# Another list of orders and engines for the operations of a Nyström attention followed by a ReLU MLP

## The chip, the cores and the metric

The kernel runs on one core of one Trainium2 chip. The metric is the device time of one execution in microseconds (us). The time before is 260.32 us, the median of three runs (260.05, 260.32 and 260.85).

## The reference

Inputs are q, k and v of shape 8 batches x 8 heads x 576 positions x 64, all float32, then a gain vector of 512 and two weight matrices, 512 x 2048 and 2048 x 512. Cut to what matters:

```python
q_lm = q.reshape(B, H, 32, 18, D).mean(axis=3)      # 32 landmarks
k_lm = k.reshape(B, H, 32, 18, D).mean(axis=3)
A  = softmax(scale * q @ k_lm^T)                    # 576 x 32
Bm = softmax(scale * q_lm @ k_lm^T)                 # 32 x 32
C  = softmax(scale * q_lm @ k^T)                    # 32 x 576
Z  = Bm^T / (norm1(Bm) * norminf(Bm) + 1e-6)
for _ in range(6):
    Z = 2 * Z - Z @ Bm @ Z
x   = A @ Z @ C @ v                                 # then heads side by side: 576 x 512
xn  = (x - mean(x)) / sqrt(var(x) + 1e-6) * g_ln
out = x + relu(xn @ w_ch1) @ w_ch2
```

## The kernel before, in words

The kernel does not issue its instructions as it builds them. Its functions record 1,649 operations (class `Op`), each with one engine or a choice of engines, in groups of batches: the start with batch 0 (operations 0 to 277), then the sets (1), (2), (3), (4, 5) and (6, 7) in `SETS`. A string `ORDER` then lists all operation numbers in the order of issue, and a string `BY` gives one letter (P for GpSimd, A for ScalarE, D for VectorE, S for SyncE's queue) for each operation that has a choice. A loop at the end issues them; each engine works through its own part of this order, and waits by semaphores for what it needs.

```python
    by = [op.by if len(op.by) == 1 else next(ways) for op in program]
    for i in order:
        program[i].issue(by[i])
```

Tiles are named buffers of a `Place` with a few slots. `Buf.place` takes the first free slot when an operation that uses the tile is issued, and `done` gives it back after the last one, so that the order of the list sets the rotation of the slots also. Loads land in `stg` (6 slots); results of matmuls stand in PSUM as `bank` (4 slots) or as `p` (pairs of banks, 2 slots).

For each batch, q, k and v come in halves (four heads each, 576 KB): a load (line 231, on SyncE's queue), a cast to fp16 on one of three engines (line 201, into `nat` for q and k, `natv` for v), and for q and k a turn, which is a transposing DMA (line 827, SyncE's queue, into `xT`). Landmarks of k come from sums of the cast tile on GpSimd (`asum`, `s`) and a small product on TensorE; landmarks of q come from reduces on VectorE over the turned tile (line 835). Then follow the scores of the landmarks, their softmax, the six iterations on 32 x 32 tiles (`st`), the scores of k and q with exponentials on ScalarE (`ect`, `ea`; `e` in the profile), their normalization by a multiplication with `lns` (e<-e,lns), and the product with v (`cv`). `zt` is the small product of the iterated matrix and `cv`; copied out of PSUM it lets TensorE form `m`, which takes the first layer of the MLP directly from `ea` (p<-e,m). The relus of the first layer (`hT`) run on ScalarE (line 210) or VectorE (line 211). Sums of hT tiles (`mix`, line 214) go to VectorE or GpSimd and feed the second layer, whose parts VectorE adds to the residual in `xblk` (line 217); stores follow on SyncE's queue.

Matmuls of one set are woven with the second layer of the set before. The operations of batch 7, which the change and the text on it speak of, are: 1294 and 1296 the loads of k, 1295 and 1297 their casts, 1298 and 1299 their turns; 1300 to 1303 and 1305 to 1308 GpSimd's sums for the landmarks of k; 1304 and 1309 TensorE's products of these; 1311 and 1313 the loads of q, 1312 and 1314 their casts, 1315 and 1316 their turns; 1317 and 1318 the reduces, 1319 the mask, 1324 the landmark scores; 1320 and 1322 the loads of v. Beside them run, for batches 4 and 5, 1001 and 1005 (e<-e,lns), 1007 and 1009 (copies of zt), 1038 and 1042 (the matmuls that need 1001 and 1005), 1057 to 1059 (copies of m), 1060 to 1075 (products p<-e,m, each with its relu). Of set (2), 481 and 483 are the loads of q, 482 and 484 their casts.

Of the kernel before, what the change touches and what calls it, by code (L numbers as in the profile page):

```python
# [20 lines left out]
def kernel(  # L21
# [1128 lines left out]
    for n, bs in enumerate(SETS):  # L1150
# [9 lines left out]
        0-1 14 2-6 9 15 52 17 10 16 18 11 19 55 21 12 20 22-23 58 25 13 24 27 26 28 61 29-30 7 32 34  # L1160
        31 40 35 41 33 36 43 37 63 38 42 8 39 45-46 44 103 47-48 104 107 66 49 53 101 108 102 109 54
# [5 lines left out]
        89 281 80 285 224 290 282 182 214 186 91 278 183 286 82 211 188 291 287-288 93 187 84 234  # L1167
# [4 lines left out]
        332 567 329 492 242 256 468 333 317 257 318 467 258 334 319 259 482 320 330 260 335-336 679  # L1172
# [3 lines left out]
        571 681 485-486 682 487 274 369 488 392 480 385 356 686 409 393 489 410 687 386 275 398 500  # L1176
        688 353 399 502 690 494 501 411 495 420 503 691 421 394 692 390 693 422 579 423 570 572 696
        698 254 705 265 683-684 697 707 496 400 699 497-499 395 890 391 706 701 504 357 522 689 505
        694 346 424 524 506 695 507 412 350 523 508-509 533 892 359 354 534 403 358 700 510 413 404
# [4 lines left out]
        438 901 583 910 556 442-443 749 902 444 547 582 704 920 596 750 911 598 597 917 445 751 554  # L1184
        446-447 439 599 588 565 922 557 548 589 448 895 449 903 549 717 569 450 715 718 709 453 550
        716 904 429 454 919 710 900 590 711-712 584 551 591 555 713 578 455 937 585 921 905 586 912
        714 456 587 906 744 926 457 558 745 719 600 720 594 939 927 721-722 603 559 419 723-724 923
# [4 lines left out]
        758 982 631 640 1266 638 981 632 767 771 942-943 768 641 763 642 764 754 637 752 647 753 646  # L1192
        755 772 759 440 648 643 760 644 990 994 761 991 649-650 645 995 653 949 996 958 651 781 959
        652 654 782-783 1265 1281 655 784 765 659 656 1267 1283 791 658 799 769 792 1270 1290 660
        657 800 1268 789 944 661 1271 790 797 1272 795 773 798 775 1273 945 662 796 1275 787 776 666
        785 663 788 669 1282 1276 786 950 960 1285 951 801 961 952 670 1284 762 953 804 954 766 793
        955 1269 770 1277 774 671 777 803 997 964 794 962 965 802 821 778 966-967 963 1286 672 811
        992 673 968 807 812 993 969-970 1274 808 1292 813 971 244 1278 676 972 805 814 973 451 1287
        822 806 462 809 667 974 817 810 975 668 823 833 818 1294 824 1288 779 835 819 780 827 820
        1279 815 826 976 825 986 816 977 834 978 828 987 1291 836 988-989 829-830 979 1293 1296 839  # L1200
# [8 lines left out]
        1325-1326 1082 1026 1093 1327-1328 1050 1030 1097 1329 1083 1051 1094 1036 1098 1095 1090  # L1209
        1044 1031 1338 1091 1084 1339 1032 1340 1099 1110 1341 1085-1086 1100 1087 1342 1334 1343  # L1210
        1336 1037 1335 1112 1102 1344 1046 1345 1337 886 1080 887 1346 1360 1081 1347 889 1109 888
        1348 1103 1361 1111 865 1362-1363 1104 875 1105 1349 1101 1354 1041 1350 1047 1106 1355 1113
# [72 lines left out]
```

## Time and profile before

| | us |
|---|---|
| median of three runs | 260.32 |
| the profiled execution | 259.61 |
| its span | 257.9 |
| TensorE (PE) busy | 248.5 (96%) |
| VectorE (DVE) busy | 201.8 (78%) |
| ScalarE (ACT) busy | 175.1 (68%) |
| GpSimd (POOL) busy | 161.8 (63%) |
| DMA engines, q1, share of 16 engines' span | 71.7% |

The span is that of the profiled instructions; the time of the profiled execution is 1.7 us more. TensorE's clock was granted at 0.999 of full speed. A row of the timeline or of the groups gives the engine, the line of the code, the operation and the tiles (out<-in); bracketed parts give the idle time ahead of it and what ended that. SPq is SyncE's queue, on which DMAs are issued in order.

### The profile page before, as it was taken

To read this page: it belongs to the slowest core of one execution; us is meant where nothing else is said; L and a number is where in the kernel's file an instruction comes from. 1 tells how busy PE (TensorE), PEld (TensorE's weight loads), DVE (VectorE), ACT (ScalarE), POOL (GpSimd) and SP (SyncE) were. 2 spreads that over 40 slices of the span, in tenths; PEclk is the share of its full clock that TensorE was granted. 3 is DMA by queue.
4 is the path that set the end of the run, shared out by engine and by line. 5 is a ranking of instruction groups with operands and counts; after the bars stand their busy time and mean duration, and the time that the engine had idled before them with its cause. 6 is when DMAs were issued, how large, how long until landed. Compare 5 with 4: busy or idle time off the path is not lost.

```text
span 257.9 us, 7929 instructions
## 1 busy us (share of the span) xinstructions
PE 248.5 (96%) x3241; PEld 178.3 (69%) x3241; DVE 201.8 (78%) x436; ACT 175.1 (68%) x298; POOL 161.8 (63%) x172
## 2 busy tenths in 40 slices
PE   7799999999999999999999899999999999999994
PEld 6644865456654668877778556768777885788882
DVE  2678997799887889898797969799768867776651
ACT  2598987998998789989879477567776434643000
POOL 6278764899999986999382592795356007406810
PEclk9999999999999999999999999999999999999999
DMA  6999999999999999999989995020060013000646
GB/s 242 378 403 397 403 409 406 351 319 294 259 296 320 276 294 360 269 253 246 214 254 267 237 191 158 22 66 3 4 142 21 4 29 75 0 3 20 159 106 185
DMA packets 51788, 53.73 MB, mean 208 GB/s; under 512 B 30628, under 2 KB 30888, under 8 KB 51752
## 3 DMA queue, kind: packets, MB, share of 16 engines
q1 hardware_dynamic: 51352, 52.70, 71.7%
q10 hardware_dynamic: 400, 0.52, 0.7%
q8 instruction: 25, 0.41, 0.6%
q14 instruction: 11, 0.09, 0.1%
HBM read 36.70 MB, written 9.44 MB: 179 GB/s over the span
## 4 chain that ended last, share of the span: by engine, by line
PE 80%; DMA 10%; POOL 5%; SPq 2%; ACT 1%; issue 1%; DVE 0%; POOLq 0%; ACTq 0%
PE bank L194 50%; PE p L194 30%; DMA stg<-in_v_dram 3%; DMA stg<-in_moe_w_ch_dram 3%; DMA stg<-in_q_dram 3%; POOL asum L214 2%; SPq L231 2%; DMA out_dram<-xblk 1%; POOL natv L201 1%; PE p L198 1%; POOL w L379 1%; POOL e L214 0%; ACT natv L201 0%; POOL nat L201 0%; ACT lns L205 0%
## 5 line engine op out<-in xcount | busy, mean ns | idle before, releaser
L194 PE MATMUL bank<-w,hT 128*128 128x256 f16 (+3 forms) x496 | 89.2, 311 | 0.0
L210 ACT ACTIVATE hT<-p 128x576 f16<-128x576 f32 x102 | 64.5, 651 | 31.1 <-PE p L194 30.6
L194 PE MATMUL p<-e,m 128*128 128x288 f16 x512 | 79.2, 286 | 0.2 <-ACT lns L205 0.2
L194 PEld LDWEIGHTS <-hT 128*128 128x128 f16 x688 | 63.7, 98 | 20.5 <-issue 3.4
L194 PEld LDWEIGHTS <-m 128*128 128x128 f16 x512 | 48.4, 98 | 17.7 <-issue 2.0
L217 DVE SCALAR_TENSOR_TENSOR xblk<-bank,rstd,xblk 128x256 f32<-128x256 f32 (+2 forms) x97 | 46.7, 506 | 16.6 <-PE bank L194 15.3
L214 POOL TENSOR_TENSOR mix<-mix,hT 128x1024 f16<-128x1024 f16 x10 | 21.6, 2169 | 22.0 <-DVE mix L214 20.0
L194 PE MATMUL bank<-stg,mix 128*128 128x256 f16 x192 | 25.4, 273 | 0.0
L549 DVE BATCH_NORM_STATS2 six<-xblk 128x6 f32<-128x512 f32 x36 | 24.4, 682 | 0.9 <-ACT xblk L201 0.9
L205 ACT ACTIVATE e<-p 128x576 f16<-128x576 f32 x32 | 19.7, 652 | 7.5 <-PE p L194 7.2
L211 DVE TENSOR_SCALAR hT<-p 128x576 f16<-128x576 f32 x26 | 19.4, 753 | 6.1 <-PE p L194 5.7
L214 POOL TENSOR_TENSOR e<-e,lns 128x576 f16<-128x576 f16 x11 | 14.4, 1316 | 15.5 <-ACT lns L205 8.4
L214 POOL TENSOR_TENSOR hT<-hT 128x1024 f16<-128x1024 f16 x6 | 12.8, 2128 | 14.9 <-DVE mix L214 14.9
L194 PEld LDWEIGHTS <-mix 128*128 128x128 f16 x192 | 18.2, 98 | 3.9 <-issue 1.3
L201 ACT COPY xblk<-bank 128x512 f32<-128x512 f32 (+2 forms) x30 | 17.0, 582 | 3.8 <-PE bank L194 3.7
L201 POOL CAST natv<-stg 128x1152 f16<-128x1152 f32 x8 | 10.4, 1310 | 11.5 <-DMA stg<-in_v_dram 8.3
L201 POOL CAST nat<-stg 128x1152 f16<-128x1152 f32 x12 | 14.2, 1196 | 4.8 <-DMA stg<-in_q_dram 3.0
L201 DVE CAST nat<-stg 128x1152 f16<-128x1152 f32 x12 | 10.4, 866 | 8.7 <-DMA stg<-in_q_dram 7.3
L835 DVE TENSOR_REDUCE qlm<-xT 128x64 f16<-128x1152 f16 x12 | 16.0, 1344 | 1.1 <-DMA xT<-nat 1.1
L214 POOL TENSOR_TENSOR asum<-asum 128x256 f32<-128x256 f32 (+1 forms) x24 | 15.4, 642 | 1.3
L214 POOL TENSOR_TENSOR asum<-nat 128x512 f32<-128x512 f16 x12 | 14.8, 1236 | 1.0 <-ACT nat L201 0.5
L201 ACT CAST m<-p 128x1024 f16<-128x1024 f32 x11 | 11.2, 1014 | 5.9 <-PE p L194 5.8
(124 smaller groups left out, 411.3 us busy)
## 6 DMA issues: line engine op xcount, KB each, us to landing
stg<-in_q_dram SPq DMA_DIRECT2D x16, 576.0 KB, 6.4
stg<-in_k_dram SPq DMA_DIRECT2D x16, 576.0 KB, 6.0
stg<-in_v_dram SPq DMA_DIRECT2D x16, 576.0 KB, 5.9
out_dram<-xblk SPq DMA_DIRECT2D x67, 128.0 KB, 3.5
stg<-in_moe_w_ch_dram SPq DMA_DIRECT2D x16, 512.0 KB, 6.8
xT<-nat SPq DMA_TRANSPOSE x24, 6.3
out_dram<-xblk ACTq DMA_DIRECT2D x3, 128.0 KB, 2.8
out_dram<-xblk ACTq DMA_DIRECT2D x1, 96.0 KB, 2.7
```

What stands on the lines that cost most here:

```text
L194: PE(lambda e, o, l, r: e.matmul(o, l, r, start=start, stop=stop, tile_position=(rb, cb), skip_group_check=(skip or cb != 0)), o, l, r)
L198: PE(lambda e, o, l, r: e.matmul(o, l, r, is_transpose=True, tile_position=(0, 0)), o, i_, idn)
L201: later(by, lambda e, o, i: e.copy(o, i) if e is nc.scalar else e.tensor_copy(out=o, in_=i), o, i)
L205: later("A", lambda e, o, i: e.activation(o, i, func, **kw), o, i)
L210: later(by, lambda e, o, i: e.activation(o, i, AF.Relu) if e is nc.scalar else e.tensor_scalar(out=o, in0=i, scalar1=0.0, scalar2=None, op ...
L211: e.tensor_scalar(out=o, in0=i, scalar1=0.0, scalar2=None, op0=ALU.max), o, i)
L214: later(by, lambda e, o, x, y: e.tensor_tensor(out=o, in0=x, in1=y, op=op), o, x, y)
L217: later("D", lambda e, o, x, s, y: e.scalar_tensor_tensor(out=o, in0=x, scalar=s, in1=y, op0=op0, op1=op1), o, x, scalar, y, hold=hold)
L231: later(by, lambda e, o, i: e.dma_start(out=o, in_=i), o, i)
L379: e.tensor_scalar(out=o, in0=i, scalar1=g, scalar2=0.0, op0=ALU.mult, op1=ALU.add),
L549: later("D", lambda e, o, i: e.bn_stats(out=o, in_=i), six, x_blk[j])
L835: later("D", lambda e, o, i: e.tensor_reduce(out=o, in_=i, axis=AX.XY, op=ALU.add), t[:, x, :], xT[x].rearrange("p j (g a) -> p g j a", a=2))
```

## The change

Only the two strings are replaced. `ORDER` lists the same 1,649 operations in another order (one line more, so that later lines count one higher), and `BY` changes the engine of 93 of them: for example 15 relus of hT go from VectorE to ScalarE and 11 the other way, 3 casts of q or k from VectorE to GpSimd and 3 back, 3 multiplications by lns from VectorE to GpSimd and 4 the other way. Its author describes it as a new list from a replay with turns placed when their issue ends, and with loads that may take buffers four places ahead. In the stretch that holds batch 7's loads of q, 1312 goes from VectorE to GpSimd, 1314 from GpSimd to ScalarE, 1005 from GpSimd to VectorE, 1007 from VectorE to ScalarE, and 1009 from ScalarE to VectorE. The core of the diff:

```diff
     ORDER = """
-        0-1 14 2-6 9 15 52 17 10 16 18 11 19 55 21 12 20 22-23 58 25 13 24 27 26 28 61 29-30 7 32 34
-        31 40 35 41 33 36 43 37 63 38 42 8 39 45-46 44 103 47-48 104 107 66 49 53 101 108 102 109 54
+        0-1 14 2-6 9 15 52 17 10 16 18 11 19 55 21 12 20 22 278 23 58 25 13 24 27 26 28 61 29-30 7
+        32 34 31 40 35 41 33 36 43 37 63 38 42 8 39 45-46 44 103 47-48 104 107 66 49 53 101 108 102
...
-        831 452 1010 1280 983 837 665 832 840 1013 984 1311 1011 841 677 985 1012 847 1014 1295 675
-        842 1289 1002 678 843 1027 848 1003 844 664 998 838 1028 1015 1313 849 1016 845 674 850 999
-        1019 1298 852-853 1297 846 854 1008 851 1006 1023 1004 1312 855 1009 856 1000 1320 1007 1017
-        859 1299 1020 860 1001 1024 1332 1021 1330 1333 858 861 1314 857 1331 862 1315 1056 866 1005
-        869 1018 1059 1057 870 1058 1300 871 1316 872 1025 1062 863 1301 1042 873 1063 1038 1070 876
-        1302 1029 868 879 1071 1303 880 877 1305 1039 1072 867 1043 1066 1073 1322 1033 1306 881
-        1067 1022 874 1034 1064 1321 1035 864 1317 1060 1065 878 1304 882 1307 1061 1076 1318 1308
-        883 1079 1068 1309 884 1319 1069 1310 1074 1077 1088 1075 1078 1324 885 1089 1040 1323 1092
+        839 1293 1296 830 677 983 831 837 1010 1311 840 985 832 668 1011 841 984 1012 674 842 1013
+        1295 847 664 844 1002 1014 848 451 1003 838 1019 665 998 843 1020 1027 849 1313 845 999 850
+        1298 1289 1028 853 851 1297 1023 1312 852 1008 1006 854 846 855 1024 1300 1299 856 1004 1009
+        859 858 1007 1000 1015 1021 860 1016 1301 1330 857 1332 1315 1005 1331 861 1302 1333 862
+        1001 1056 1314 869 1059 1058 870 1303 1316 871 1057 1305 872 866 863 1072 876 1306 1038 1073
+        1070 1017 1320 879 1307 1322 873 1071 1042 1039 1308 865 1064 1043 880 1317 864 1065 1033
+        1062 875 878 881 1034 1063 1025 1060 877 1304 1066 1035 1061 874 1318 882 1067 1309 1068
+        1310 883 1069 1319 884 1018 1076 1022 1324 1074 1077 1079 1321 1029 885 1325 1090 1075 1036
...
     BY = """
-        PPPPPAAPPPPPPPDPPPPDPPDPADAAPAAAPADDDAAADDADADPADAAAADDAADDAADADDAADDAAAADADAAPPADAAAADDAD
-        DPDADAAADAAAADDAAAADADAAAAAAAADDDDDPDPDPADDDAAAAAAAAADPAAAAAAADAAAAAAAAAAAAAAAAAAAAADDPPPD
-        DDAPADDAPAPAPAAPPPPPDAAAAADDAADDAADAAAAAADADDAAAAAAAAADPPPPPDPDDADAADDAAAADAAAAAAAADPDDPDD
-        DPPPDDPAAAADDPPPPPPPADADDADADAAADDAAAADDDADADAAAAAADDADDPPPDDDADAAAAAADAAADADAADAADADDPPDP
-        PPSSASSSAASASA
+        PPPPPAAPPPPPPPDPPPPPPPDAADAAPAAAPADDADADADAAAPDDDDDAADDAAADAADAADAADDAAAADADAAPDAPAAAADDAD
+        DPPADADADADAADAAAADDADAAAAAAAAAADDDPPPDDADDDAAAAAAAAAPPAAAAAAAAAAAAAADAAAAAAAAAAAAAADDPPPD
+        DDAAADPAAPDADDAPPPPDADAAAADDDAADAADAAAAAAAADAAAAAAAAADDPPPPDPDDDAAAADAADADDAAAAAAAAADDDDPD
+        PPPPADPAAAAAPAPPPDPDAADAAADDAADADDAAADAADADADAADDDADAADDPPPPPDAAADADAADAADAAADAAAAAADDPPPD
+        DDASASSAASSASA
     """
```

More of the change, by code (lines that the diff above doesn't have):

```diff
@@ L1195 @@
[L1195 to L1199, printed above, removed]
@@ new lines @@
+        1359 1386 1052 1173 1370 1130 1385 1174 1388 1167 1371 1126 1168 1163 1387 1128 1389 1164
+        1372 1127 1397 1131 1390 1373 1169 1122 1132 1170 1045 1376 1134 1393 1377 1135 1049 1133
+        1171 1398 1165 1378 1172 1136 1394 1053 1145 1166 1374 1137 1379-1380 1382 1375 1146 1381
+        1383 1054 1159 1175 1160 1138 1177-1178 1161 1176 1147 1162 1142 1193 1055 1139 1181 1194
+        1391 1140 1148 1182-1183 1144 1149 1195 1152 1141 1184-1185 1392 1153 1179 1186 1154 1196
+        1180 1430 1143 1197 1207 1151 1433 1191 1431 1150 1201 1432 1192 1187 1395 1412 1188-1189
@@ new lines @@
+        1209 1198 1190 1401 1200 1446 1402 1208 1434 1447 1420 1199 1202 1435 1403 1203 1210 1442
+        1204 1212 1443 1213 1205 1220 1440 1206 1438 1421 1441 1214 1396 1413 1439 1215 1436 1211
+        1221 1437 1450 1222 1452-1453 1216 1219 1444 1451 1218 1223 1217 1462 1445 1224 1463 1227
+        1226 1228 1399 1454 1400 1458 1225 1455 1407 1229 1409 1230 1459-1460 1408 1233 1231 1456
+        1404 1232 1405 1234 1457 1235-1236 1461 1448 1483 1243 1529 1237 1487 1244 1240 1449
+        1245-1246 1253 1247 1485 1468 1250 1249 1254 1469 1251 1255 1530 1256 1238 1532 1471 1252
@@ new lines @@
+        1257 1406 1464 1248 1258 1465-1466 1410 1259 1467 1260 1414 1531 1472 1411 1261 1473 1541
+        1484 1416 1542 1537 1422 1488 1474 1417 1538 1547 1418 1477 1548 1424 1476 1543 1425 1486
+        1415 1475 1478 1544 1479-1480 1419 1426 1533 1470 1545 1534 1489 1481 1490 1495 1482 1491
[3 rows of a table added]
+        1520 1586 1560 1263 1521-1522 1515 1581 1569 1518 1526 1583 1570 1523 1239 1571-1572 1517
+        1575 1573 1242 1576 1574 1585 1527 1577-1578 1241 1587 1580 1524 1588 1579 1262 1589 1593
+        1590 1528 1595 1591 1596 1592 1597 1594 1598 1601 1599 1602 1600 1603-1604 1607 1606 1608
@@ L1238 @@
+        1605 1609-1610 1617 1614 1618 1611 1615-1616 1619 1612 1620 1627 1621 1628 1624 1629 1622
+        1630 1625 1631 1626 1632 1623 1525 1633-1634 1613 1638-1639 1635 1640-1645 1637 1636 1646
+        1648 1647
     """
     BY = """
[L1240 to L1242 removed]
```

41 lines of the change are left out of this document (11 added, 30 removed), and 70 rows, old and new, of the table ORDER.

## The prediction

> **What bounds the kernel now.** I read the page first (engine shares), then the windows, then the waits, and last the timeline around the largest wait.
>
> ```profile
> span 257.9 us, 7929 instructions
> PE 248.5 (96%) x3241; PEld 178.3 (69%) x3241; DVE 201.8 (78%) x436; ACT 175.1 (68%) x298; POOL 161.8 (63%) x172
> ```
>
> TensorE (PE) works 96% of the span. The other engines have room on average, so what a reordering can win is mostly the time in which TensorE stands still. The windows say where that is (columns: window, its length, then busy time and instructions of each engine, granted clock, DMA share, GB/s).
>
> ```profile
> core 0: us, PE busy (x) PEld busy (x) DVE busy (x) ACT busy (x) POOL busy (x), PEclk, DMA share, GB/s
> 25.00:140.00 115.00, 115.00 (x1565) 77.87 (x1562) 101.45 (x215) 100.63 (x173) 92.05 (x89) 1.00 1.07 307
> 140.00:145.00 5.00, 3.86 (x78) 3.13 (x62) 3.41 (x6) 3.73 (x8) 1.28 (x1) 1.00 1.11 224
> 145.00:150.00 5.00, 4.88 (x51) 3.23 (x50) 4.57 (x10) 2.40 (x5) 4.07 (x4) 1.00 1.06 232
> 150.00:155.00 5.00, 4.93 (x60) 2.58 (x58) 3.48 (x6) 3.76 (x7) 4.61 (x8) 1.00 1.19 192
> 155.00:160.00 5.00, 4.69 (x43) 3.41 (x44) 4.93 (x14) 3.31 (x8) 1.42 (x2) 1.00 0.61 191
> 180.00:210.00 30.00, 29.85 (x318) 23.38 (x317) 22.86 (x43) 18.73 (x32) 9.91 (x6) 1.00 0.16 37
> 237.00:257.90 20.90, 17.02 (x156) 14.43 (x154) 9.21 (x20) 0.65 (x1) 6.32 (x3) 0.99 0.58 145
> ```
>
> From 25 to 140 us TensorE has no gap at all. From 140 to 160 it lacks 1.14 + 0.12 + 0.07 + 0.31 = 1.64 us, from 180 to 210 another 0.15. The last window's 3.88 us are the time after the last matmul. The start, up to 25 us, has its own waits:
>
> ```profile
> engine line waited for: us in total, times, longest us
> PE bank L194 <- DVE zeros L254: 1.5, 1, 1.5
> PE p L198 <- DVE nat L201: 1.2, 2, 0.9
> PE p L194 <- DVE zt L201: 1.1, 1, 1.1
> PE bank L194 <- POOL s L214: 0.4, 1, 0.4
> ```
>
> Zeros and nat belong to the start. The zt row and the s row are the gaps of 140 to 160 us. Their causes, row by row, from the timeline (columns: start, length, engine, line, operation, tiles, count, and in brackets the idle time before it and what ended it):
>
> ```profile
> 133.17 2.07 SPq L231 DMA_DIRECT2D out_dram<-xblk  x2
> 135.34 0.54 SPq L231 DMA_DIRECT2D stg<-in_q_dram  x1
> ...
> 141.54 1.28 POOL L214 TENSOR_TENSOR e<-e,lns 128x576 f16<-128x576 f16 x1 [5.12 <-ACT lns L205]
> 141.90 1.55 DVE L201 CAST nat<-stg 128x1152 f16<-128x1152 f32 x1 [1.59 <-DMA stg<-in_q_dram]
> ...
> 143.37 0.28 DVE L201 CAST zt<-p 128x128 f16<-128x128 f32 x1
> 143.70 0.47 PE L194 MATMUL p<-qbd,xT 128*64 128x64 f16 x18 [1.14 <-DVE zt L201]
> ```
>
> The load of batch 7's first q half (operation 1311) is issued at 135.34; its cast (1312) starts on VectorE at 141.90, 6.56 us later. VectorE had been idle for 1.59 us, and behind the cast stands the small copy of zt (1007), which alone would free the p bank that TensorE needs. The matmul waits 1.14 us. The second half (1313) does the same to GpSimd. The chain of waits has its transfer and cast, the timeline what follows:
>
> ```profile
> 138.65 7.05 DMA stg<-in_q_dram
> 145.85 1.14 POOL nat L201
> ```
>
> ```profile
> 148.19 1.16 POOL L214 TENSOR_TENSOR asum<-nat 128x512 f32<-128x512 f16 x1
> 149.43 1.26 POOL L214 TENSOR_TENSOR asum<-asum 128x256 f32<-128x256 f32 x2
> ...
> 155.31 0.20 PE L194 MATMUL bank<-pm,s 128*128 128x64 f16 x1 [0.39 <-POOL s L214]
> ```
>
> GpSimd's cast 1314 starts at 145.85; the sums for k's landmarks (1300 to 1308) come after it, and TensorE waits 0.39 us for the last one.
>
> **The change, part by part.** *TensorE's own work*: the same operations in another order. Laid end to end, each order changes between whole-array and smaller matmul shapes equally often, so I cost this at nothing; bounds −0.2 to +0.2 us. *Start and end*: in the new lists what TensorE waits for up to about 22 us stands as it did (one reduce of VectorE, 278, comes some 10 us sooner), and the last matmuls, normalizing steps and stores as well: nothing.
>
> *The gap at 143.70.* In the new lists 1312 goes to GpSimd, the two zt copies change places (1007 to ScalarE, 1009 to VectorE). VectorE no longer has a cast of a fresh load ahead of zt. ScalarE has no such cast there either: 1314, which it receives, stands behind 1007. So 1.14 us go. What is late next: GpSimd. On SyncE's queue only one store (677) instead of two now stands between the k load (1296) and load 1311; one of the two rows of 133.17 is about 1.0 us. I estimate the issue at 133.9 to 134.5. With the same 6.56 us the data land at 140.4 to 141.0. GpSimd then casts (1.2 to 1.55), does three sums (1.16 + 1.26) and the multiplication e·lns (operation 1001, 1.28): done at 145.3 to 146.5. The matmuls that need it (1038) stand in the new order where TensorE would be at about 146.7. The 1.14 us have a cover of 0.2 to 1.4 us.
>
> *The gap at 155.31 and the small ones.* The sums 1300 to 1308 are queued ahead of everything that waits for 1313: they end some 3 us before their matmuls. 0.39 us go, of which 0.31 lie in the window. The 0.12 at 145 to 150 was TensorE waiting for an e·lns (1005) on GpSimd, which goes to VectorE; its own duration is in a row below. Together with the first I take 1.53 us (bounds 1.14 to 1.64, plus 0.15 at 180 us if it goes too: 1.79).
>
> *What is given back: 1314 and the turns of batch 7.* Four kinds of rows price it, from the timeline of SyncE, ScalarE and VectorE:
>
> ```profile
> 143.47 7.29 SPq L827 DMA_TRANSPOSE xT<-nat  x3
> ...
> 145.56 1.07 ACT L201 CAST m<-bank 128x512 f16<-128x512 f32 x2 [0.70 <-PE bank L194]
> 148.10 0.65 ACT L210 ACTIVATE hT<-p 128x576 f16<-128x576 f32 x1 [1.47 <-PE p L194]
> ...
> 153.01 2.61 DVE L835 TENSOR_REDUCE qlm<-xT 128x64 f16<-128x1152 f16 x2 [0.77 <-DMA xT<-nat]
> 155.66 0.42 DVE L214 TENSOR_TENSOR qbd<-qlm,mask2x 128x256 f16<-128x256 f16 x1
> ```
>
> 1314 now waits for its load on ScalarE, and stands in the list where ScalarE would be at about 143.9. The load is issued 0.3 to 1.3 us sooner than before (138.65), landing at 144.4 to 145.4 with 7.05 us. Behind it on ScalarE: two casts of m (1.07 us) and two relus (0.65 each) that free p banks. From 145.4: cast 1.14 (GpSimd's row, as bound), m 1.07, relus 1.3 gives 148.9, against a matmul (1064) at about 148.1 that wants the bank: 0.8 late; from 144.4 it is in time. The turns 1315 and 1316 now follow each other without a load between; the three of the row took 2.4 us each on the queue. VectorE's reduce 1317 stands at about 148.5, the turn lands at 149 to 150.5; after 2.61 + 0.42 the landmark scores start at 152.0 to 153.5 against 153.7 in the order: covered by 0.2 to 1.7. Both together: 0 to 1.4, I take 0.35, near the lower end, since the covers hold for the middle of each estimate.
>
> *The casts elsewhere.* Set (2)'s q loads (481, 483) are issued later:
>
> ```profile
> 40.25 2.39 SPq L231 DMA_DIRECT2D stg<-in_q_dram  x2
> ...
> 48.18 0.75 DVE L201 CAST nat<-stg 128x1152 f16<-128x1152 f32 x1
> ```
>
> In the new list they stand some 1.7 us further down, so that 481 leaves SyncE at about 42.0 instead of 40.25, and its cast 482 goes to GpSimd, where it would be wanted at about 48.3. With 6.56 to 7.05 us it lands at 48.6 to 49.0, so the cast starts 0.3 to 0.7 late, and an e·lns multiplication is queued behind it. That is 0 to 0.5 us; I take 0.15, because TensorE had no gap at all there. Some 85 other operations change engine; relus of hT between ScalarE and VectorE (11 one way, 15 the other) and mixes of hT between VectorE and GpSimd (7 and 8) are the most, and they lie mostly where TensorE had no gap: 0, bounds 0 to +0.5.
>
> *The shared port.* e·lns (1005) goes to VectorE beside GpSimd's sums:
>
> ```profile
> L214 DVE TENSOR_TENSOR e<-e,lns 128x576 f16<-128x576 f16 x3 | 2.8, 923 | 0.0
> ```
>
> By this row it costs 0.92 us on VectorE and nothing on GpSimd, and I take that. But the cast at 141.90 took 1.55 us while GpSimd multiplied (141.54 to 142.82), and the one at 48.18 took 0.75: the two engines may take turns. If GpSimd's sums had to wait for 1005, its chain would end 0.92 us later, at 146.2 to 147.4, against the 146.7 at which TensorE wants it: 0 to 0.7 us.
> The Trainium skill, page "SBUF — State Buffer", section "Who interferes with whom", says that VectorE operations with two SBUF inputs and GpSimd's reads share a port pair under an exclusive lock, and that the loser waits for the whole instruction. It speaks against moving 1005 beside the sums; the pair 1.55 against 0.75 agrees with it, and by it the sum would be that of the third rival.
>
> **Sum.** Against the profiled execution's own 259.61 us (span 257.9 and 1.7 around it): −1.53 + 0.35 + 0.15 = −1.03, so 258.6. The median of the runs is 260.32, 0.71 above the profiled one; the same difference gives **259.3**.
>
> **The rivals.**
> 1. *The wait only moves* (chance 0.15). Load 1311 lands no sooner than before (141.9), because SyncE's stores ahead of it are held by their producers. Then GpSimd ends 1001 at 141.9 + 1.55 + 2.42 + 1.28 = 147.2 against 146.7, and everything behind it is late by 0.5; 1314 on ScalarE gives back 0.6. Gain 1.53 − 1.1 − 0.15 = 0.3: about 260.0. For it: the queue is in order, and store issues of 0.5 to 1 us stand beside each load. Against it: the bare count of stores fell.
> 2. *Late loads cost more than the gap* (chance 0.30, slower). The place is ScalarE's 1314: if load 1313 lands at 146.5 (issued as late as before and taking 1 us more among the denser turns), ScalarE runs 2.1 us behind, p banks come 1.9 us late, turn 1316 cannot be issued before the cast, and the reduces and landmark scores are 0.5 to 1 late; the early q loads of set (2) give 0.5. 1.9 + 0.9 + 0.5 − 1.53 = +1.8: 262.1; it is slower than before from a landing at about 145.7, as late as before, if the rest follows in proportion. For it: planned times from issue to use in the new list, laid beside TensorE's work, are 4.6 to 6.2 us for these q loads, less than the measured 6.56 and 7.05. Against it: the old list was as short (5.2 to 5.4), and lost only 1.64 us by it.
> 3. *GpSimd and VectorE take turns* (chance 0.10) at 1005 and the sums: 0.7 late, 260.0. For it: the pair of casts. Against it: 1005 may fall beside GpSimd's wait for load 1311.
>
> **How the numbers follow.** A run of this kernel can be told from no change at about 0.3%, or 0.78 us. The forecast (0.45) is faster by 1.0; rivals 1 and 3 give within 0.3%: 0.25; rival 2 slower: 0.30. Low end: 1.79 us gone, nothing given back, 0.2 for TensorE's order and 0.1 of scatter: 258.2. High end: rival 2 at 262.0.
>
> **What would show it.** Right: no TensorE wait on zt near 143 and none on s near 155; the q load issued at about 134, cast on GpSimd at about 140.5 to 141; TensorE's idle time from 140 to 160 under 0.7 us, still full from 60 to 140. Wrong: a wait of TensorE on a p bank behind ScalarE's relus near 148 (rival 2), on e·lns near 147 (rival 1), GpSimd's sums near 143 well over 1.2 us (rival 3), or new gaps before 140 us at places that I costed at nothing.

## The result, and the profile after

The changed kernel is slower: 263.31 us median of 22 runs (261.09 to 267.4) against 260.86 for the kernel before (259.61 to 263.75, 22 runs beside it on the same chips). The ratio of the undisturbed runs is 1.0081, with a 95% interval of 1.0054 to 1.0108, which is 2.1 us (1.4 to 2.8). The forecast was 259.3, the range 258.2 to 262.0. Its profiled execution took 261.60 us with a span of 259.9, 2.0 us more than the one of before. The intervals below are 95% intervals of the same kind of ratio, each against runs of before in the same session; a ratio between two edited kernels is worked out from two such ratios.

TensorE's share is unchanged, its instructions as many as before (page of the changed kernel):

```profile
PE 249.6 (96%) x3241; PEld 179.6 (69%) x3241; DVE 201.3 (77%) x433; ACT 176.9 (68%) x305; POOL 156.7 (60%) x168
```

The windows of the changed kernel (columns as before):

```profile
25.00:140.00 115.00, 111.65 (x1514) 74.64 (x1512) 97.98 (x203) 96.51 (x170) 90.81 (x89) 1.00 1.07 299
140.00:145.00 5.00, 5.00 (x61) 4.25 (x60) 4.65 (x11) 4.94 (x9) 0.64 (x1) 1.00 0.92 271
145.00:150.00 5.00, 5.00 (x87) 3.81 (x85) 3.98 (x6) 4.44 (x8) 4.53 (x5) 1.00 1.12 267
150.00:155.00 5.00, 5.00 (x53) 3.42 (x52) 5.00 (x11) 3.70 (x7) 3.70 (x6) 1.00 1.16 131
155.00:160.00 5.00, 5.00 (x55) 2.80 (x53) 4.46 (x12) 3.91 (x8) 1.42 (x1) 1.00 1.01 360
```

In this profile the gaps after 140 us are gone, all 1.79 us of them (from 180 to 210 us, too, TensorE is busy throughout). From 25 to 140 us, where the profile of before had no gap, TensorE now lacks 3.35 us. Its waits there, from the timeline of TensorE:

```profile
63.70 0.76 PE L194 MATMUL p<-qbd,xT 128*64 128x64 f16 x36 [0.57 <-DVE qbd L214]
85.37 0.38 PE L194 MATMUL bank<-zcbd,e 128*128 128x256 f16 x2 [0.90 <-DVE m L201]
89.29 1.01 PE L194 MATMUL p<-qbd,xT 128*64 128x64 f16 x36 [0.45 <-ACT hT L210]
100.01 0.66 PE L194 MATMUL p<-e,m 128*128 128x288 f16 x4 [0.33 <-DVE m L201]
108.98 0.24 PE L194 MATMUL bank<-cv,st 32*32 32x64 f16 x8 [1.01 <-ACT st L201]
```

At the waits at 85, 89, 100 and 109 us the engine named was not busy too long. It stood still itself, for a load, with the small operation that TensorE wanted queued behind the load's cast (timelines of VectorE and ScalarE, in order of time):

```profile
83.96 0.76 DVE L201 CAST nat<-stg 128x1152 f16<-128x1152 f32 x1 [2.15 <-DMA stg<-in_q_dram]
84.64 0.68 DVE L201 CAST m<-bank 128x512 f16<-128x512 f32 x1
...
87.53 1.17 ACT L201 CAST natv<-stg 128x1152 f16<-128x1152 f32 x1 [2.50 <-DMA stg<-in_v_dram]
88.60 1.18 ACT L210 ACTIVATE hT<-p 128x576 f16<-128x576 f32 x2
...
98.59 0.76 DVE L201 CAST nat<-stg 128x1152 f16<-128x1152 f32 x1 [1.16 <-DMA stg<-in_k_dram]
99.27 0.68 DVE L201 CAST m<-bank 128x512 f16<-128x512 f32 x1
...
107.12 1.17 ACT L201 CAST natv<-stg 128x1152 f16<-128x1152 f32 x1 [1.42 <-DMA stg<-in_v_dram]
108.19 0.64 ACT L205 ACTIVATE e<-p 128x576 f16<-128x576 f32 x1
108.72 0.21 ACT L201 CAST st<-bank 128x64 f16<-128x64 f32 x1
```

It is the picture of the old gap at 143.70 (a cast ahead of zt), in other places. At 63.7 us it was a turn that VectorE had stood 0.61 us for. The loads are those of batches 4 and 5: 907 (q), 916 (v), 922 (k) and 946 (v). SyncE's queue shows where they lose time. Before:

```profile
78.88 0.53 SPq L231 DMA_DIRECT2D stg<-in_v_dram  x1
79.51 2.15 SPq L827 DMA_TRANSPOSE xT<-nat  x1
81.76 0.58 SPq L231 DMA_DIRECT2D stg<-in_v_dram  x1
```

and in the changed kernel:

```profile
82.16 0.53 SPq L231 DMA_DIRECT2D stg<-in_v_dram  x1
82.79 4.76 SPq L827 DMA_TRANSPOSE xT<-nat  x2
87.66 0.52 SPq L231 DMA_DIRECT2D stg<-in_v_dram  x1
...
98.96 2.44 SPq L231 DMA_DIRECT2D out_dram<-xblk  x4
101.50 0.53 SPq L231 DMA_DIRECT2D stg<-in_v_dram  x1
```

The first load in both is 916, the last of the first three rows is 918: issued at 81.76 before and at 87.66 after, since two turns (894, 895) stand ahead of it instead of one. Load 946 is issued at 101.50, at 95.06 before, behind eight stores that the new list gathers there.

### The profile page after: what moved, and what is told of

It is laid out like the page before. It is cut to its first block, busy times and chain, and to the rows that moved or that the text cites. A ratio compares the mean times of both kernels' runs of the same rounds, so it can differ in the third digit from the quotient of the medians.

```text
span 259.9 us, 7915 instructions
## 1 busy us (share of the span) xinstructions
PE 249.6 (96%) x3241; PEld 179.6 (69%) x3241; DVE 201.3 (77%) x433; ACT 176.9 (68%) x305; POOL 156.7 (60%) x168
## 4 chain that ended last, share of the span: by engine, by line
PE 74%; DMA 15%; SPq 4%; POOL 2%; ACT 2%; issue 1%; DVE 1%; ACTq 0%
PE bank L194 47%; PE p L194 26%; DMA stg<-in_v_dram 7%; DMA xT<-nat 6%; SPq L231 4%; DMA stg<-in_moe_w_ch_dram 2%; POOL w L379 2%; PE p L198 1%; ACT hT L210 1%; ACT natv L201 1%; DVE qlm L835 1%; POOL natv L201 0%; SPq L827 0%; ACT e L205 0%; DVE qbd L214 0%
## 5 line engine op out<-in xcount | busy, mean ns | idle before, releaser
L210 ACT ACTIVATE hT<-p 128x576 f16<-128x576 f32 x106 | 66.9, 650 | 30.1 <-PE p L194 29.1
L214 POOL TENSOR_TENSOR mix<-mix,hT 128x1024 f16<-128x1024 f16 x9 | 19.5, 2165 | 17.1 <-DVE mix L214 17.0
L214 POOL TENSOR_TENSOR hT<-hT 128x1024 f16<-128x1024 f16 x8 | 16.9, 2121 | 11.6 <-DVE mix L214 11.6
L201 POOL CAST nat<-stg 128x1152 f16<-128x1152 f32 x11 | 12.8, 1168 | 16.9 <-DMA stg<-in_q_dram 9.5
L194 PEld LDWEIGHTS <-mix 128*128 128x128 f16 x192 | 18.2, 98 | 4.3 <-issue 1.9
L211 DVE TENSOR_SCALAR hT<-p 128x576 f16<-128x576 f32 x22 | 16.4, 751 | 6.1 <-PE p L194 4.9
L201 DVE CAST nat<-stg 128x1152 f16<-128x1152 f32 x13 | 11.6, 890 | 8.5 <-DMA stg<-in_q_dram 6.3
L201 POOL CAST natv<-stg 128x1152 f16<-128x1152 f32 x7 | 8.6, 1228 | 12.7 <-DMA stg<-in_v_dram 12.5
L201 ACT COPY xblk<-bank 128x512 f32<-128x512 f32 (+1 forms) x27 | 15.8, 590 | 0.5 <-PE bank L194 0.3
L214 POOL TENSOR_TENSOR hT<-hT,mix 128x1024 f16<-128x1024 f16 x4 | 8.5, 2126 | 12.5 <-PE bank L194 12.5
L194 PEld LDWEIGHTS <-e 64*64 64x64 f16 (+2 forms) x392 | 11.5, 104 | 6.1 <-issue 2.8
```

Of the source, the lines that this page charges most:

```text
L194: PE(lambda e, o, l, r: e.matmul(o, l, r, start=start, stop=stop, tile_position=(rb, cb), skip_group_check=(skip or cb != 0)), o, l, r)
L201: later(by, lambda e, o, i: e.copy(o, i) if e is nc.scalar else e.tensor_copy(out=o, in_=i), o, i)
L210: later(by, lambda e, o, i: e.activation(o, i, AF.Relu) if e is nc.scalar else e.tensor_scalar(out=o, in0=i, scalar1=0.0, scalar2=None, op ...
L211: e.tensor_scalar(out=o, in0=i, scalar1=0.0, scalar2=None, op0=ALU.max), o, i)
L214: later(by, lambda e, o, x, y: e.tensor_tensor(out=o, in0=x, in1=y, op=op), o, x, y)
```

## Experiments

**Which part of the lists.** The two lists have issued nearly the same operations by their 856th place (each has by then three that the other has not), near 118 us. So they can be joined there, both ways.

```diff
 # before_then_after
-ORDER, BY: those of one list throughout
+ORDER, BY: before's for the first 856 operations, the changed kernel's for all others
 # after_then_before
+ORDER, BY: the changed kernel's for the first 856 operations, before's for all others
```

> Order and engines of before for the first 856 operations (to about 118 us), of the changed kernel for the rest. If the changed kernel's loss lies wholly in the gaps of TensorE from 63 to 110 us and its gain in the gaps after 140 us (both theories of the loss say so), TensorE has no gap over 0.4 us from 25 us on, and the kernel is 1.5 to 2.2 us faster than before (about 258.5). If the gain after 140 us only came because TensorE was already late there (loads had more time), the gap near 143 us comes back, 1 us or more, and the time is within 0.8 us of before.

> The reverse: the changed kernel's lists for the first 856 operations, before's for the rest. If the two parts are independent, it has the gaps of both: 4.2 us from 60 to 115 and about 2.2 after 140, so 2 us slower than the changed kernel (about 4 slower than before). If the late start of the second part gives its loads time, the gap near 143 us is under 0.4 us and it is as long as the changed kernel.

Measured: before_then_after 0.9969 (0.9931 to 1.0006), so 0.8 us faster than before at the middle (0.2 slower to 1.8 faster); after_then_before 1.0129 (1.0074 to 1.0183), 3.4 us slower. With the changed kernel's own 1.0081, the new first part costs 2.9 us (1.7 to 4.1) beside the new second part and 3.4 (1.9 to 4.8) beside the old one. The new second part gains 0.8 us (from a loss of 0.2 to a gain of 1.8) and 1.2 (from a loss of 0.4 to a gain of 2.8), which is not clear of nothing. So the loss lies in the first part, whichever second part follows.

The gaps did not split as cleanly as the times. after_then_before has before's second part, and its profile has no wait on zt near 143 us; after 140 us it lacks 0.4 us in all. And before_then_after did not keep the old first part free of gaps, though that part is the same to the letter:

```profile
PE p L194 <- DVE hT L211: 1.5, 1, 1.5
PE bank L194 <- DVE qbd L214: 0.6, 1, 0.6
PE p L194 <- DVE qbd L214: 0.3, 1, 0.3
```

(These are its waits of TensorE from 25 us on.) The row of 1.5 us lies at 87.8 us, in a stretch where the profile of before had none. So the next question was how far one profile can be trusted.

**Second profiles of both kernels, nothing edited.**

> The kernel before, unchanged, profiled a second time. If its stretch from 25 to 140 us has slack, TensorE has no gap over 0.2 us there again. If the absence of gaps in the first profile was only just so (loads landing a little sooner than their casts are wanted), gaps of 0.4 to 2 us in sum stand at the places where the edited kernels showed them: near 63.5 us (wait on qbd) and near 88 us (wait on VectorE's hT).

> The changed kernel, unchanged, profiled a second time. If the list makes the gaps, four of the five (near 64, 85, 89, 100 and 109 us) stand again, in sum 3 us or more, at the same instructions. If they were chance landings of that one execution, they stand elsewhere or sum to under 2 us.

These two executions were long, 265.81 and 266.58 us, and single, so their times are not compared. The places of the gaps can be read. TensorE's waits from 25 to 140 us, first the kernel before:

```profile
PE p L194 <- DVE hT L211: 2.5, 1, 2.5
PE p L194 <- DVE qbd L214: 1.5, 1, 1.5
PE bank L194 <- DVE xblk L217: 1.1, 1, 1.1
```

then the changed kernel:

```profile
PE bank L194 <- ACT st L201: 2.3, 1, 2.3
PE p L194 <- DVE qbd L214: 1.9, 1, 1.9
PE p L194 <- ACT hT L210: 0.6, 1, 0.6
```

The kernel before has gaps near 64.6 and 89.9 us (qbd, hT) after all, at the places named in advance, and more of them than expected (0.4 to 2 us). Its first profile, at 259.61 us, was the fastest of the 22 runs. Of the changed kernel's five places, three stand again (qbd, hT and st), one less than expected; those on m nearly vanished. The waits sum to 5.1 us in the old list and to 4.8 in the new one, so in these executions TensorE's gaps do not tell the two lists apart: the cost of the first part rests on the times of the joined lists. The first part has no cover in either list. The wait for st is in both profiles of the changed kernel and in neither of before, but after_then_before, with the same list there, has none.

The second profile of before shows one thing more. After 140 us it has only these waits:

```profile
PE bank L194 <- POOL e L214: 0.4, 1, 0.4
PE bank L194 <- POOL s L214: 0.4, 1, 0.4
```

The wait of 1.14 us on zt is not there. Seven of the profiles in this document have before's second part, and it stands in the first of them alone; the other six lose 0 to 1.0 us after 140 us, 0.56 in the mean. Of the profiles with the changed kernel's second part, its engines included, eleven beside the first lose 0.2 to 1.4 us there, 0.6 in the median, nearly all of it in a wait on qbd between 156 and 170 us. So the largest gap that the change was expected to close was one of a single execution.

**SyncE's order, or the engines?**

```diff
 # sync_order_before: the changed kernel, its DMAs from 45 to 120 us
-SyncE: 679 485 681 469 486 696 698 705 684 683 707 265 890 ...
+SyncE: 679 469 681 485 486 696 698 254 705 265 683 684 707 ...
 # engines_before: the changed kernel
-BY: the new letters
+BY: before's letters
```

> The changed kernel, with the DMAs that SyncE issues from 45 to 120 us put back in before's relative order; TensorE, ScalarE, VectorE and GpSimd keep the changed kernel's order and engines. Theory queue (loads and turns come late because of the order of SyncE's queue): loads 907, 916, 922 and 946 are issued 2 to 6 us sooner, the gaps at 85, 89, 100 and 109 us together fall from 3.5 to under 1 us, and the kernel is 2.5 to 4 us faster than the changed one. Theory engines (casts given to engines that cannot wait): the gaps stay over 2.5 us and the time within 1 us of the changed kernel's.

> The changed kernel's order, every operation on the engine that it has in before. Theory queue: loads land as late as in the changed kernel, whatever engine casts them, so gaps of 3 us or more stay between 60 and 115 us (their places may move), and the time is within 1.5 us of the changed kernel's or longer. Theory engines: the gaps from 60 to 115 us fall under 1 us and it is 2.5 us or more faster.

Both missed, and neither tells the theories apart. sync_order_before came out at 1.018 (1.0035 to 1.0324): the old order of DMAs against the new order of casts made a new wait of its own (ScalarE stood 5.97 us for a buffer that a turn still read, TensorE 5.46 us for a relu behind it). engines_before came out at 1.0536 (1.0461 to 1.061): six waits for VectorE's relus, 6.8 us in sum. An order and its engines belong together; taken apart, they make larger gaps than those under study. The edits from here on move a few DMAs only.

**Loads ahead of stores, turns apart.**

```diff
 # loads_first: the changed kernel
-SyncE: ... 701 243 266 907 244 909 254 916 894 ... 911 255 452 429 937 430 939 419 440 418 441 946 924 925
+SyncE: ... 701 907 909 916 243 266 244 254 894 ... 911 937 939 946 924 255 452 429 430 419 440 418 441 925
 # turns_apart: the changed kernel
-SyncE: ... 684 683 707 265 890 276 ... 700 701 243 266 907 244 909 ... 894 895 918 920 912 922 911 255 452 429 ... 924 925 941 948
+SyncE: ... 684 707 265 890 276 683 ... 700 243 266 907 244 909 701 ... 894 918 920 895 912 922 255 452 429 911 ... 924 941 948 925
 # before_stores_first: the kernel before
-SyncE: ... 700 243 255 907 418 909 277 276 916 ...
+SyncE: ... 700 243 255 277 276 266 907 418 909 916 ...
```

> The changed kernel with two edits on SyncE's queue: loads 907, 909 and 916 go ahead of the four stores 243, 266, 244 and 254, and loads 937, 939, 946 and turn 924 go ahead of the eight stores from 255 to 441. All other engines keep their order. Theory queue: 907 is issued 1.3 us and 916 some 3 us sooner, 946 about 2 us sooner; the gaps at 85 and 89 us (1.9 us together) fall under 0.6 and the one at 109 us (1.1) under 0.3; the kernel is 1.5 to 2.5 us faster than the changed one, about 260.5 to 261.5. Rival (the DMA engines are full, so an earlier issue only takes longer to land): the loads land within 0.7 us of where they do in the changed kernel, and the gaps stay over 2.5 us.

> The changed kernel, with the second turn of each close pair (683, 701, 895, 911, 925) moved one to three loads or stores further down SyncE's queue; the stores ahead of the loads stay. If a turn's issue is long (3.0 to 4.0 us) because the turn ahead of it is still in flight, the five of them take 1.3 to 2.9 us, together some 5 us less, the loads 918, 946 and 948 are issued 2 to 4 us sooner, and the gap at 109 us goes, a gain of 0.5 to 2 us over the changed kernel. If a turn's issue is long for another reason (full DMA engines), the five still take over 15 us together and nothing is gained.

> Both edits together (701 behind load 916, 937, 939, 946 and 924 behind store 452). Theory queue: no gap over 0.5 us from 70 to 115 us; 2.5 to 4 us faster than the changed kernel, so 0 to 1.5 us faster than before. Rival (full DMA engines): within 1 us of the changed kernel.

> The kernel before with one edit: the three stores 277, 276 and 266 go ahead of load 907 on SyncE's queue. Nothing else moves. Theory queue with no cover (a stretch without a gap of TensorE has no slack either): 907 and 909 land 1 to 2 us later, their casts hold VectorE, and TensorE gets a gap of 0.5 to 1.5 us between 84 and 90 us; the kernel is 0.5 to 1.5 us slower than before. If the stretch had slack, as the prediction had it (0 us for what is moved there), the time is within 0.4 us of before.

loads_first did what it was to do on the queue (916 at 78.73, 946 at 98.53), and the waits at 85, 89 and 109 us went. The time did not: 1.0142 (1.0055 to 1.0228). TensorE's waits from 25 to 140 us are:

```profile
PE bank L194 <- DVE xblk L217: 1.3, 1, 1.3
PE p L194 <- DVE qbd L214: 1.0, 1, 1.0
PE p L194 <- DVE m L201: 0.4, 1, 0.4
```

Those for qbd (63.7 us, ahead of what was moved) and for m (99.2) are the changed kernel's own. The 1.3 us is new, at 113.7 us: VectorE stood 2.58 us for turn 941, which now leaves behind the eight stores (issued at 108.40), and the addition into xblk is queued behind that turn's reduce. The loads did land sooner than in the changed kernel, 907 by 3.2 us, 916 by 2.1 and 946 by 4.2. So the rival that full DMA engines only make an earlier issue take longer failed too, and so did the gain of 1.5 to 2.5 us. The waits of this profile do not explain why the time is longer.

turns_apart missed, at 1.0295 (1.0236 to 1.0354). Turn 701, moved behind loads 907 and 909, held up a reduce and with it TensorE for 5.5 us. It is telling on the issue of turns all the same: the five moved ones took 10.0 us together instead of 17.8, as expected, but the other six of the stretch (684, 700, 894, 912, 924 and 941) 18.2 instead of 10.3. Two of these, 912 and 941, now stand directly behind another turn. Both edits together gave 1.0522 (1.0462 to 1.0582), with the same wait (7.6 us).

before_stores_first came out as expected in its time: 1.0051 (1.0007 to 1.0096), 1.3 us slower (0.2 to 2.5) from three stores put ahead of loads 907 and 909, two of them by three places and 266 by seventeen. Its one wait is of 2.9 us, on hT at 88.3 us. The kernel before, unedited, waits 2.5 us for hT there in its second profile, so the time speaks for the edit and that wait does not. By the time, the old list has no slack there.

**What resource.** Two edits take away stores of the same stretch, one with their issue, one without.

```diff
     for i in order:
+        if i in skipped:                 # no_stores: 14 stores, 265 to 441
+            for b in program[i].bufs:
+                b.done()
+            continue
+        if i in small_stores:            # small_stores: the same 14; before_small_stores: 14 of before's
+            program[i].calls = [(w, [a[0:1] for a in args], kw) for w, args, kw in program[i].calls]
         program[i].issue(by[i])
```

> The changed kernel without the 14 stores that SyncE issues from 67 to 101 us (those rows of the output are not written). It takes away 10 us of issue on SyncE's queue and 1.8 MB from the DMA engines. If the loads are late because of the queue or of the DMA engines, both of these theories say that the gaps between 80 and 115 us (3.7 us) fall under 0.8 and that the kernel is 2.5 to 4 us faster than the changed one. If the loads are held by something else (buffers that casts free), the gaps stay over 2 us.

> The changed kernel in which the same 14 stores are issued but write one row each (the other rows of those blocks are not written). The issues stay, 0.5 to 0.6 us each, the bytes go. If SyncE's issue time makes the loads late, the gaps between 80 and 115 us stay over 2.5 us and the time within 1 us of the changed kernel's. If the DMA engines' time does (a store of 128 KB lands 0.37 us behind the one before it, 14 of them 5.2 us), the gaps fall nearly as far as without the stores, to under 1.3 us.

> The kernel before in which the 14 stores that SyncE issues from 58 to 110 us write one row each (the other rows of those blocks are not written). If before too is held in that stretch by the time of the DMA engines, in those executions where loads land late, its median falls by 0.5 to 1.5 us. If before has slack there, its time stays within 0.4 us.

no_stores came to 1.0017 (0.9981 to 1.0053) and small_stores to 0.9994 (0.9959 to 1.0029): against the changed kernel's 1.0081 that is 1.7 us (0.5 to 2.8) and 2.3 us (1.1 to 3.4) less, the first of them less than the 2.5 to 4 that were expected. Keeping the issues and dropping the bytes is worth as much as dropping both. In no_stores the waits at 85, 89 and 109 us are gone (TensorE's waits from 25 to 140 us; the first lies at 64 us, ahead of the stores, the second at 99):

```profile
PE p L194 <- DVE qbd L214: 1.3, 1, 1.3
PE p L194 <- DVE m L201: 0.5, 1, 0.5
```

In small_stores the waits from 80 to 115 us sum to 0.2 us; one of 3.1 us, on qbd at 67.0 us, lies ahead of the stores. But its 14 issues did not stay as they were: together they took 10.0 us of SyncE's queue in the changed kernel and 4.2 us here, 0.72 and 0.30 us each. The 4.2 us that are left cost nothing that can be seen. That speaks for the time of the DMA engines, not SyncE's issue time, as what makes the loads late, and does not show it, since 5.8 us of issue went with the bytes. The Trainium skill, page "DMA: Bandwidth & Descriptors", section "Issuing engines are not separate DMA queues", says that all DMAs end up on the same 16 engines and interleave there, and that issuing from several engines saves only sequencer time; by that, moving the stores to another engine's queue would have saved their issue time alone. No run here tests another queue.

before_small_stores came to 0.9926 (0.9886 to 0.9966), 1.9 us (0.9 to 3.0) less than before, where 0.5 to 1.5 was expected. The old list is held by its stores nearly as hard, so their bytes do not set the two lists apart.

Three more edits tried to use this.

```diff
 # before_loads_first: the kernel before; before_then_after_loads: the same edit in before_then_after
-SyncE: ... 243 255 907 418 909 277 276 916 894 ...
+SyncE: ... 907 909 916 243 255 418 277 276 894 ...
 # stores_later: the changed kernel
-SyncE: ... 937 430 939 419 440 418 441 946 ... 942 277
+SyncE: ... 937 939 419 946 ... 942 430 440 418 441 277
```

> The kernel before with five stores (243, 255, 418, 277, 276) moved behind load 916 on SyncE's queue; nothing else moves. Loads 907, 909 and 916 land 0.5 to 1.5 us sooner, which gives the stretch at 85 to 88 us a cover. In before's profile TensorE had no gap there, so by the gaps of that profile nothing is gained (within 0.4 us); if the scatter of before's times comes from this place, the median falls by 0.3 to 1 us and the range of its times narrows.

> Before's lists for the first 856 operations, the changed kernel's for the rest, and the same five stores behind load 916. No gap of TensorE over 0.5 us from 70 us on; 258.0 to 259.0, that is 1.5 to 2.5 us faster than before. If the earlier loads only move the wait to the turns 894 and 911 behind the stores, a gap of over 0.8 us comes between 88 and 100 us and the time is that of the plain joined lists (259).

> The changed kernel with the four stores 430, 440, 418 and 441 moved behind turn 942 on SyncE's queue; nothing else moves. Theory DMA engines' time: load 946 and the turns 924 and 925 land 1.5 to 2.5 us sooner, the gap at 109 us (1.1 us) falls under 0.4, the gaps at 64, 85 and 89 us stay; 0.5 to 1.3 us faster than the changed kernel. Rival (the wait only passes on to what stands behind the stores, as with the loads put first): a new gap of 0.8 us or more between 110 and 125 us, no gain.

The first gained nothing, 1.001 (0.9971 to 1.005), the second 1.0029 (0.9997 to 1.0061): in the profile of before_then_after_loads the five stores now stand ahead of turn 894 and loads 918 and 920, ScalarE waits 2.64 us for 920 with klm behind its cast, and TensorE 1.6 us for klm near 94 us. That is the second branch of its expectation, though at the middle 0.6% slower than the plain joined lists. stores_later came to 1.0331 (1.0227 to 1.0436). The wait at 109 us hardly fell (0.8), and the late stores kept their xblk buffers; ScalarE stood for one, and TensorE 8.3 us for an lns behind it:

```profile
120.50 0.58 ACT L201 COPY xblk<-bank 128x512 f32<-128x512 f32 x1 [8.82 <-DMA out_dram<-xblk]
```

**The turns that moved up.** In the three profiles with before's unedited first part, load 918 is issued at 81.8, 83.7 and 84.1 us; in the three with the changed kernel's, where 894 and 895 are ahead of it, at 87.7, 88.6 and 89.3. Three turns stand further up in the new list: 895, 912 and 925. Two edits move these, one in each direction; the second also puts turn 911 ahead of load 922. With the turns, some nat and xT buffers get other slots in turn.

```diff
 # before_turns_ahead: the kernel before
-SyncE: ... 916 894 918 920 911 922 895 429 937 912 939 419 946 924 266 463 430 941 948 925 1264
+SyncE: ... 916 894 895 918 920 911 912 922 429 937 939 419 946 924 925 266 463 430 941 948 1264
 # after_turns_behind: the changed kernel
-SyncE: ... 916 894 895 918 920 912 922 911 255 452 429 937 430 ... 946 924 925 941 948 1264
+SyncE: ... 916 894 918 920 911 922 895 255 452 429 937 912 430 ... 946 924 941 948 925 1264
```

> The kernel before with three turns moved to where the changed list has them, ahead of loads: 895 directly behind turn 894 (so ahead of loads 918 and 920), 912 ahead of load 922, 925 directly behind turn 924. Nothing else moves. If these turns are the part of the new list that costs, load 918 is issued at 84.5 us or later instead of 81.8 to 84.1, load 922 at 89 or later instead of 86.6 to 88.2, gaps come between 88 and 115 us, and the kernel is 1 to 3 us slower than before. If they do not matter, the time is within 0.5 us of before.

> The changed kernel with the same three turns put back behind loads as in before (895 behind load 922, 911 ahead of 922, 912 behind load 937, 925 behind load 948). If they are the part that costs, load 918 is issued at about 84.8 us instead of 86.9 to 89.3, the gaps near 100 and 109 us (1.6 us) fall under 0.6, those near 64, 85 and 89 us stay, and the kernel is 0.8 to 2.5 us faster than the changed one (1.0081 of before), so within 1.000 +- 0.005 of before. If not, it stays slower than before by 1.5 us or more.

In their times both went the way of the theory. before_turns_ahead: 1.0087 (1.0042 to 1.0132), 2.3 us (1.1 to 3.4) slower than before. On its queue (timeline of SyncE) the second turn now holds the loads as in the changed kernel:

```profile
79.22 0.53 SPq L231 DMA_DIRECT2D stg<-in_v_dram  x1
79.85 6.19 SPq L827 DMA_TRANSPOSE xT<-nat  x2
86.14 0.54 SPq L231 DMA_DIRECT2D stg<-in_v_dram  x1
```

Load 918 goes at 86.14, and 922 at 93.35, behind turns 911 and 912, which take 6.0 us. Load 920 lands at 93.16 us (90.12 in the first profile of before) and 922 at 98.08 (92.60). Their casts on ScalarE and GpSimd wait for them:

```profile
93.22 1.15 ACT L201 CAST nat<-stg 128x1152 f16<-128x1152 f32 x1 [1.76 <-DMA stg<-in_k_dram]
...
98.23 1.14 POOL L201 CAST nat<-stg 128x1152 f16<-128x1152 f32 x1 [1.75 <-DMA stg<-in_k_dram]
```

TensorE then waits 0.74 us at 94.59 for klm, which is queued behind the first of these casts, and 1.21 us at 101.97 for s, behind the second. Its third wait, 1.1 us on hT at 86.8 us, is at a place where the unedited kernel waits too.

after_turns_behind: 1.0031 (0.9999 to 1.0063), which is 1.3 us (0.2 to 2.4) faster than the changed kernel's 1.0081. Load 918 is issued at 83.27, and the wait at 100 us is gone. The wait near 108 us is not; it is 2.3 us in this profile, where 946 still stands behind the eight stores (100.74). The waits from 25 to 140 us sum to 3.3 us, as in the changed kernel's profile, so that the gain shows in the times alone. The expectation held for the time and for 918, and failed for that gap.

These turns cannot have made the waits at 85 and 89 us, since they stand behind loads 907 and 916. And one rival is left untested: five casts of the stretch (910, 919, 921, 923 and 938) changed engine as well, so that a late load holds another engine than before. The cast of load 918 went from GpSimd to ScalarE, and that of 922 from GpSimd to VectorE, ahead of m. engines_before put all engines back at once, which is too coarse to weigh this.

No kernel here that writes the whole output is clearly faster than before. before_then_after is the nearest, and its interval reaches 1.0006.

## Why the prediction was wrong

*Removal of the gaps after 140 us (−1.53 us, bounds to −1.79):* as forecast in the changed kernel's first profile, where all went, the 0.15 near 181 us too; TensorE had no wait on zt and none on s. But 1.14 us of it was the wait on zt that six other profiles of before's second part do not have, so the term was sized from one execution. The joined lists give the second part 0.8 and 1.2 us, neither clear of nothing, against a forecast of 1.18 (1.53 less the 0.35 below). The cast that went to GpSimd waited 4.68 us there for its load and held nobody up, as the cover said:

```profile
145.32 1.14 POOL L201 CAST nat<-stg 128x1152 f16<-128x1152 f32 x1 [4.68 <-DMA stg<-in_q_dram]
146.42 1.16 POOL L214 TENSOR_TENSOR asum<-nat 128x512 f32<-128x512 f16 x1
...
146.78 1.40 DVE L214 TENSOR_TENSOR e<-e,lns 128x576 f16<-128x576 f16 x1
```

The times of issue in this stretch (q load at 134, cast at 140.5 to 141) were wrong by 4.5 us; 3.35 us of that are TensorE's gaps ahead.

*Given back at 1314 and the turns (0.35 us):* 0 in the changed kernel's first profile, 0.6 in before_then_after. Over the eleven other profiles of the new second part it is 0.2 to 1.4 us, 0.6 in the median. TensorE waits there for qbd, and not for ScalarE's relus. The size was about right, the wait another one.

*The shared port (third rival):* the multiplication that went to VectorE took 1.40 us beside GpSimd's sums, against the 0.92 that the sum used. It cost TensorE nothing there.

*The step that failed* is "they lie mostly where TensorE had no gap: 0, bounds 0 to +0.5", with the 0.15 for set (2)'s loads. It measured 3.35 us in the profile, 2.9 and 3.4 by the joined lists. Two errors are in it. First, no gap in one execution was taken for slack. It was the fastest execution of 22, and a second profile shows 5.1 us of gaps in the same stretch. Three stores moved ahead of two loads there cost 1.3 us. Second, only the engines of the operations were weighed in that stretch, not the places of its DMAs; SyncE's queue was followed only from 132 us on. Three turns moved ahead of loads cost 2.3 us in the kernel before and explain about 1.3 us in the changed one.

*The second rival* named the mechanism, late loads whose casts hold ScalarE and VectorE, but at 1314, with one of its q loads. It happened at 85 to 109 us, with loads 907, 916, 922 and 946, and through turns and stores ahead of them. The profile of before held a sign for a higher chance than its 0.30: DMA share was 1.05 to 1.13 in every 10 us from 25 to 125 us.

*Open:* after_turns_behind leaves 0.8 us (0 to 1.6) to before, and about as much again that the second part should gain. The eight stores ahead of 946 and the engines of the casts are the likely places. loads_first put 946 ahead of these stores and stores_later moved four of them, but both made new waits of their own, and no run changes those casts alone, so that this stays open. How much of the cost stands in TensorE's gaps is open too, since the gaps of single profiles vary as much as the two lists differ.

## What to carry to other kernels

A stretch in which one profile shows TensorE without a gap is not a stretch with slack, and a gap of one profile is no surer: the wait on zt was in one profile of seven. Profile the kernel a second time, or move a few stores there, before an edit is costed at nothing or a gap is counted as a gain. In these kernels the loads landed in the order of SyncE's queue. A turn of 4.0 us moved ahead of load 918 let it go 4.4 us later and land 3.3 us later, and the loss showed as a wait for the small operation queued behind a late load's cast. Orders and engines that were found together should be joined with others only at places where both have done the same work.

## What the runs showed of the hardware

A turn's issue holds SyncE for 1.30 us at the least (the turn at 91.79 in before), but the second of two in a row for up to 4.3 us (912 in before_turns_ahead). A load between two is not always enough: 895 took 3.38 us in before. Setting turns apart did not lower the sum over the eleven of the stretch (28.2 us in turns_apart against 28.1 in the changed kernel).

A gap costs more than itself when it is long. In the second profile of before, 2.5 us without a matmul were followed by a granted clock of 0.67 in the next window, and the matmuls there took longer:

```profile
85.00:90.00 5.00, 2.47 (x16) 1.39 (x15) 3.99 (x5) 2.60 (x4) 4.54 (x5) 0.99 1.17 286
90.00:95.00 5.00, 5.00 (x57) 2.59 (x56) 3.03 (x6) 2.44 (x5) 3.19 (x4) 0.67 1.10 303
```

By the stretch itself, the clock was 0.50 for 3.4 us (89.86 to 93.27). The gap of 1.5 us in before_then_after was followed by a clock of 1.00. Over the waits of TensorE between 25 and 240 us in all profiles of this document, each of the ten of 2.2 us or more was followed by such a stretch, two of the four between 1.8 and 2.2 us were, and no shorter one. The Trainium skill, page "TensorE: Matmul & The Clock Gate", Part 1, puts the drop to half rate behind an idle window of about 3.4 us; here one of 2.5 us was enough, and by the starts of its matmuls the slow ones cost another 1.5 us.

VectorE's qbd took 1.41 us at 85.66 in before_then_after, while GpSimd multiplied e·lns for 1.88 us, and 0.39 us in the profile of before. In before, qbd had started at 84.28, before GpSimd's multiplication at 84.39. In before_then_after the relu hT stands behind qbd, and TensorE's wait of 1.5 us is for it.
